# A quarter of W_out between W_in's chunks, v ahead of q for batch 1, and a new order of steps, in a packed attention and MLP kernel

## The chip, the cores and the metric

The kernel runs on one core of a Trainium2 chip. The metric is the device time of one execution in microseconds (us). The core has a matrix engine (TensorE, "PE" in the profile; its weight loads are "PEld"), a vector engine (VectorE, "DVE"), an activation engine (ScalarE, "ACT"), GpSimd ("POOL") and a queue engine (SyncE, "SP"). Each takes its instructions in the order of the program and waits by semaphores for the others. Loads from device memory go through 16 DMA engines, which all queues share.

## The reference

Two attentions stand one after the other, then an MLP. In the first attention 32 packed queries per head read 576 keys and values; in the second the 576 queries read the 32 results, as keys and as values. The heads are put side by side and go through the MLP with a squared Relu.

```python
def sm_attn(qq, kk, vv):
    s = scale * np.matmul(qq, kk.transpose(0, 1, 3, 2))
    ...
    return np.matmul(a, vv)
p_packed = sm_attn(p, k, v)
out = sm_attn(q, p_packed, p_packed)
...
h = x @ w_in
r = np.maximum(h, 0.0)
g = s * (r * r) + b
return (g @ w_out).astype(np.float32)
```

Batch 8, heads 8, sequence 576, head size 64; x has 4608 rows of 512; W_in is 512 x 2048 and W_out 2048 x 512. Inputs and output are float32.

## The kernel before

Matmuls run in bf16; the loads on GpSimd's queue convert from float32 as they go. The eight batches are worked off one after another, but their steps are mixed: while the attention of batch b + 1 runs, the last product of batch b fills the gaps of TensorE. The mixing is written out by hand, as a list of words (lines 663 to 690) that `run` (line 569) turns into calls. All instructions are pinned: the order of the words is the order on every engine. What the words mean, with their functions:

- `Lk`, `Lq`, `Lv`, `Lp`, `Lwi`, `Lwo`: issue a load on GpSimd's queue (lines 115 to 143). `Lwi0` to `Lwi3` are the four chunks of W_in, of 512 columns each; `Lwo0` to `Lwo3` the four quarters of W_out, each four of its 16 blocks of rows. One is 512 KB in bf16, a batch's k, q or v 576 KB. k, q and v have one raw buffer each, so batch 1's may come only when batch 0's has been read.
- `Tk b.h`, `Tq b.h` (`on_pe`, line 189): transpose half of the heads of k or q on TensorE, then copy to SBUF. For batches 2 to 7 `Dk` and `Dq` do it by a DMA of SyncE's queue.
- `V` (`order_v`, line 220): DVE reorders v. `F b.a` (`first_scores`): first scores of half of the heads, and Exp on ACT. `P` (`packed`): their product with v, then a reciprocal and two scalings on DVE. `X` (`turned`): transposes the result, `ppd`.
- `S` (`second_scores`), `A b.x` (`weights`, and `weights_half` for batch 0): second scores, Exp, sums by a matmul with ones, Ln, Exp of minus that, and the product on DVE that gives aT. For batch 0 this last product is the word `G` (line 340), by halves of the rows.
- `W b.c` (`packed_w`, line 356): ppd times chunk c of W_in (for later batches two chunks), which is the MLP's first weight with the second attention's values folded in. It is copied from PSUM to `pw` by ACT (first part) and DVE (second part). For batch 0's chunk 0 DVE copies it in two halves, the second at the word `E`.
- `M b.m` (`mlp_in`, line 430): 4 matmuls aT times block m of pw, a Relu to `rlu` (on ACT; on DVE for batch 0 where m % 4 == 2), and the square to gT on DVE. `h 0.m.f` (`mlp_in_half`) is the same for two blocks and half of the rows; h0.0.0 has its Relu on DVE.
- `O b.t x n` (`Out.step`, line 498): n of the 16 matmuls of an output tile of 128 rows, gT times a block of W_out. Step m needs gT's block m and W_out's quarter m // 4. After the sixteenth DVE scales it and adds the bias, and SyncE stores it.
- `BT`, `BC` (lines 462 and 477): column sums of W_out for the bias; BT reads all four quarters. `PA`, `PPA`: the same preparation of p for batches 2 to 7 at once; `PD`, `PP` for one batch.
- `Z n` and `Y n`: fillers, n matmuls of 512 columns on a tile of zeros. `Z` (line 551) writes to a PSUM tile of its own, `Y` (line 558) to the buffer that the next step will use.

PSUM: the steps T, PP, F, S, A, M, h, BT, BC and W of later batches share two buffers of two banks (`psh`, tag h, shown as `hps`); a step may start only when the copy or Relu of the step two before has read its buffer. O, P, Z and W of batch 0 share four buffers of one bank.

The order of the opening's loads on GpSimd's queue before the change, behind batch 0's k, p, v and q: `Lwi0 Lwi1 Lwi2 Lwi3 Lwo0 Lwo1 Lp1 Lk1 Lq1 Lv1 Lwo2 Lwo3 Lpall Lk2`.

Of the kernel before, what the change touches and what calls it, by code (L numbers as in the profile page):

```python
# [14 lines left out]
def kernel(  # L15
# [45 lines left out]
    def mm(*a, **kw):  # L61
        return tc.keep_in_program_order(nc.tensor.matmul(*a, **kw))  # L62
# [367 lines left out]
    def mlp_in(b, m):  # L430
        hps = big()
        for a in range(2):
            for hf in range(2):
# [7 lines left out]
        rlu = ysp.tile([P, 2, HS], BF16, tag="rlu", name="rlu")
        if b == 0 and m % 4 == 2:
            vec.tensor_scalar_max(out=rlu[:], in0=hps[:, :, 0:HS], scalar1=0.0)
        else:
            act.activation(out=rlu[:], in_=hps[:, :, 0:HS], func=AF.Relu)
# [1 line left out]
        vec.tensor_tensor(
            out=gT[:, m, g0:g0 + S].rearrange("p (a s) -> p a s", a=2),
            in0=rlu[:], in1=rlu[:], op=ALU.mult,
        )  # L450
# [212 lines left out]
    for word in """
        Lwi0 Lwi1 Lwi2 Lwi3 Lwo0 Lwo1 Lp1 Tk0.0 Z10 PD Tk0.1 Lk1 PP0 Z3 F0.0 V0.0 F0.1 Z5 P0.0 V0.1 P0.1
        Z2 Tq0.0 Z1 X0 Z1 Tq0.1 Lq1 Lv1 Lwo2 Lwo3 Lpall Z4 S0 Z3 A0.0 W0.0 Z1 A0.1 G0.0 E Z1 h0.0.0 W0.1
        G0.1 h0.2.0 Y2 h0.0.1 h0.2.1 W0.2 M0.4 W0.3 M0.5 M0.6 O0.0x1 M0.7 O0.0x3 M0.8 M0.9 O0.1x1 PD1
        O0.0x1 M0.10 M0.11 O0.0x3 O0.1x1 PP1 M0.12 O0.1x2 Tk1.0 Tk1.1 Lk2 O0.1x2 M0.13 O0.1x1 F1.0
        O0.1x1 Tq1.0 O0.2x1 Tq1.1 O0.2x1 F1.1 O0.2x2 V1 Lv2 Lq2 M0.14 P1.1 M0.15 O0.2x3 O0.0x2 X1 O0.0x2
        O0.1x1 S1 O0.1x3 O0.2x1 BT PA A1.0 O0.0x3 BC A1.1 O0.1x3 O0.2x3 W1.0 O0.0x1 O0.1x1 O0.2x5 W1.2
        V2 O0.3x6 M1.0 PPA M1.1 M1.2 Dq2 Dk2 Lk3 Lv3 Lq3 O0.3x9 M1.3 M1.4 O0.3x1 O1.0x1 M1.5 M1.6 O1.0x2  # L670
        M1.7 M1.8 O1.0x2 M1.9 M1.10 O1.0x2 M1.11 M1.12 O1.0x2 M1.13 M1.14 O1.0x2 M1.15 O1.0x2 F2.0 F2.1
        O1.0x3 O1.1x3 P2.1 O1.1x5 X2 O1.1x3 S2 O1.1x4 A2.0 O1.1x1 O1.2x1 A2.1 O1.2x7 W2.0 O1.2x8 O1.3x1
        V3 O1.3x1 W2.2 O1.3x6 M2.0 O1.3x1 M2.1 O1.3x1 M2.2 O1.3x1 M2.3 Dq3 Dk3 Lk4 Lv4 Lq4 O1.3x1 M2.4
        O1.3x1 M2.5 O1.3x1 M2.6 O1.3x1 M2.7 O1.3x1 M2.8 O1.4x1 M2.9 O1.4x1 M2.10 O1.4x1 M2.11 O1.4x1
        M2.12 O1.4x1 M2.13 O1.4x1 M2.14 O1.4x1 M2.15 O1.4x9 O2.0x6 F3.0 F3.1 O2.0x6 P3.1 O2.0x4 O2.1x1
        X3 O2.1x5 W3.0 O2.1x6 W3.2 O2.1x4 O2.2x2 S3 O2.2x4 A3.0 O2.2x2 V4 A3.1 O2.2x8 O2.3x8 M3.0 M3.1
        Dq4 Dk4 Lk5 Lv5 Lq5 O2.3x2 M3.2 M3.3 O2.3x2 M3.4 M3.5 O2.3x2 M3.6 M3.7 O2.3x2 M3.8 M3.9 O3.0x2
        M3.10 M3.11 O3.0x2 M3.12 M3.13 O3.0x2 M3.14 M3.15 O3.0x8 F4.0 F4.1 O3.0x2 O3.1x4 P4.1 O3.1x5 X4
        O3.1x3 S4 O3.1x4 A4.0 O3.2x2 A4.1 O3.2x7 W4.0 O3.2x7 O3.3x2 V5 W4.2 O3.3x6 M4.0 O3.3x2 M4.1 M4.2
        O3.3x2 M4.3 Dq5 Dk5 Lk6 Lv6 Lq6 O3.3x4 M4.4 M4.5 O3.4x2 M4.6 M4.7 O3.4x2 M4.8 M4.9 O3.4x2 M4.10  # L680
        M4.11 O3.4x2 M4.12 M4.13 O3.4x2 M4.14 M4.15 O3.4x6 O4.0x6 F5.0 F5.1 O4.0x6 P5.1 O4.0x4 O4.1x1 X5
        O4.1x5 S5 O4.1x4 A5.0 O4.1x2 A5.1 O4.1x4 O4.2x3 W5.0 O4.2x7 V6 O4.2x5 W5.2 O4.2x1 O4.3x5 M5.0
        M5.1 O4.3x2 M5.2 Dq6 Dk6 Lk7 Lv7 Lq7 M5.3 O4.3x2 M5.4 M5.5 O4.3x2 M5.6 M5.7 O4.3x2 M5.8 M5.9
        O4.3x2 M5.10 M5.11 O4.3x1 O5.0x1 M5.12 M5.13 O5.0x2 M5.14 M5.15 O5.0x12 F6.0 F6.1 O5.0x1 O5.1x5
        P6.1 O5.1x5 X6 O5.1x3 S6 O5.1x3 O5.2x1 A6.0 O5.2x2 A6.1 O5.2x7 W6.0 O5.2x6 O5.3x3 V7 W6.2 O5.3x6
        M6.0 O5.3x2 M6.1 M6.2 O5.3x2 M6.3 Dq7 Dk7 M6.4 O5.3x2 M6.5 M6.6 O5.3x1 O5.4x1 M6.7 M6.8 O5.4x2
        M6.9 M6.10 O5.4x2 M6.11 M6.12 O5.4x11 M6.13 M6.14 O6.0x2 M6.15 O6.0x5 F7.0 F7.1 O6.0x6 P7.1
        O6.0x3 O6.1x2 X7 O6.1x4 S7 O6.1x4 A7.0 O6.1x2 A7.1 O6.1x4 O6.2x3 W7.0 O6.2x12 W7.2 O6.2x1 O6.3x5
        M7.0 M7.1 O6.3x2 M7.2 M7.3 O6.3x2 M7.4 M7.5 O6.3x2 M7.6 M7.7 O6.3x2 M7.8 M7.9 O6.3x2 M7.10 M7.11
        O6.3x1 O7.0x1 M7.12 M7.13 O7.0x2 M7.14 M7.15 O7.0x13 O7.1x16 O7.2x16 O7.3x16 O7.4x16  # L690
    """.split():
# [31 lines left out]
```

## Time and profile before

| what | value |
|---|---|
| time, median of 5 runs (lowest to highest) | 250.99 us (250.51 to 251.53) |
| the profiled execution | 250.56 us |
| its span from first to last instruction | 248.8 us |
| TensorE busy | 239.1 us (96%) |
| DVE busy | 144.3 us (58%) |
| ACT busy | 138.9 us (56%) |
| fillers to their own tile (zps), in the mean 435 ns as shown | 43, 13.0 us |
| granted TensorE clock, mean | 0.998 |

Busy time is what the records cover. A matmul's end is modelled and the next one starts before it: 512 columns are shown as some 380 ns, while six of them in a row start 0.216 us apart. So a step is best priced by the starts of what comes before and after it. The idle time before an instruction stands in brackets in the timeline, with what ended it. The chain that ended last lies on TensorE for 86% of the span, on DMAs for 10%.

### The profile page before, as it was taken

To read this page: it belongs to the slowest core of one execution; us is meant where nothing else is said; L and a number is where in the kernel's file an instruction comes from. 1 tells how busy PE (TensorE), PEld (TensorE's weight loads), DVE (VectorE), ACT (ScalarE), POOL (GpSimd) and SP (SyncE) were. 2 spreads that over 40 slices of the span, in tenths; PEclk is the share of its full clock that TensorE was granted. 3 is DMA by queue.
4 is the path that set the end of the run, shared out by engine and by line. 5 is a ranking of instruction groups with operands and counts; after the bars stand their busy time and mean duration, and the time that the engine had idled before them with its cause. 6 is when DMAs were issued, how large, how long until landed. Compare 5 with 4: busy or idle time off the path is not lost.

```text
span 248.8 us, 5498 instructions
## 1 busy us (share of the span) xinstructions
PE 239.1 (96%) x2291; PEld 132.3 (53%) x2291; DVE 144.3 (58%) x278; ACT 138.9 (56%) x218; POOL 29.1 (12%) x43
## 2 busy tenths in 40 slices
PE   7796999999999999999999999999999999999994
PEld 2452566356643665356544655466545654366453
DVE  4438768498629573567548662677347642767221
ACT  2156743558846882568655763678375844577000
POOL 8633212000300030000300030001200000000000
PEclk9999999999999999999999999999999999999999
DMA  3999999999498869429898969368995911121133
GB/s 32 198 206 206 203 204 206 195 218 209 83 205 188 196 109 220 105 56 140 152 220 177 206 80 222 89 127 134 171 232 144 145 42 45 42 46 42 42 87 86
DMA packets 59450, 35.50 MB, mean 143 GB/s; under 512 B 32160, under 2 KB 54944, under 8 KB 59424
## 3 DMA queue, kind: packets, MB, share of 16 engines
q0 software_dynamic: 25184, 18.61, 50.1%
q1 hardware_dynamic: 34192, 16.49, 29.3%
q8 instruction: 18, 0.29, 0.5%
q14 instruction: 8, 0.07, 0.1%
q10 hardware_dynamic: 48, 0.03, 0.0%
HBM read 37.23 MB, written 9.44 MB: 188 GB/s over the span
## 4 chain that ended last, share of the span: by engine, by line
PE 86%; DMA 10%; ACT 1%; DVE 1%; issue 0%; POOLq 0%
PE yps L62 49%; PE hps L62 31%; DMA vn<-in_v_dram 8%; DMA kn<-in_k_dram 2%; PE zps L62 2%; PE pps L62 2%; PE hps L65 1%; PE pps L65 1%; ACT e L73 1%; DVE vr L73 0%; DVE aT L73 0%; ACT pbd L73 0%; ACT rcd L73 0%; ACT ld L73 0%; PE tps L65 0%
## 5 line engine op out<-in xcount | busy, mean ns | idle before, releaser
L62 PE MATMUL yps<-w_out_sb,gT 128*128 128x512 bf16 (+1 forms) x592 | 146.1, 374 | 0.3 <-DMA w_out_sb<-in_moe_w_out_dram 0.3
L73 ACT ACTIVATE rlu<-hps 128x576 bf16<-128x576 f32 x124 | 75.6, 649 | 28.7 <-PE hps L62 25.9
L62 PEld LDWEIGHTS <-gT 128*128 128x128 bf16 x592 | 54.8, 98 | 49.5 <-issue 7.4
L62 PE MATMUL hps<-aT,pw 128*128 128x288 bf16 x512 | 76.4, 286 | 2.4 <-DVE aT L73 2.3
L73 DVE TENSOR_TENSOR gT<-rlu 128x576 bf16<-128x576 bf16 x128 | 58.0, 458 | 31.1 <-ACT rlu L73 27.5
L62 PEld LDWEIGHTS <-pw 128*128 128x128 bf16 x512 | 49.4, 97 | 29.6 <-issue 4.5
L73 DVE SCALAR_TENSOR_TENSOR ysb<-yps,svec,biasrep 128x512 f32<-128x512 f32 (+1 forms) x37 | 26.9, 732 | 22.4 <-PE yps L62 19.3
L73 ACT ACTIVATE e<-hps 96x768 bf16<-96x768 f32 (+2 forms) x34 | 21.8, 693 | 29.9 <-PE hps L62 29.7
L73 ACT CAST pw<-hps 128x1024 bf16<-128x1024 f32 x14 | 14.2, 1012 | 16.5 <-PE hps L62 16.0
L73 DVE TENSOR_TENSOR aT<-e,rcd 128x576 bf16<-128x576 bf16 x16 | 12.1, 757 | 18.0 <-ACT rcd L73 18.0
L73 POOL DMA_DIRECT2D kn<-in_k_dram x9 | 6.9, 767 | 129.5 <-DMA kT<-kn 100.5
L73 DVE CAST pw<-hps 128x1024 bf16<-128x1024 f32 x14 | 17.0, 1217 | 2.7 <-PE hps L62 2.7
L62 PE MATMUL zps<-zb 128*128 128x512 bf16 x43 | 13.0, 435 | 1.2 <-DVE zb L73 1.2
L73 ACT ACTIVATE ld<-hps 128x576 f32<-128x576 f32 x16 | 10.3, 643 | 2.3 <-PE hps L62 1.6
L73 ACT ACTIVATE rcd<-ld 128x576 f32<-128x576 f32 x16 | 10.9, 683 | 0.5
L62 PEld LDWEIGHTS <-ppd 64*32 64x32 bf16 x384 | 3.6, 89 | 10.3 <-issue 6.9
L62 PE MATMUL hps<-w_in_sb,ppd 64*32 64x512 bf16 x224 | 8.8, 381 | 0.0
L73 DVE RECIPROCAL rd<-pps 128x2 f32<-128x2 f32 x8 | 1.4, 170 | 12.6 <-PE pps L62 12.6
L62 PEld LDWEIGHTS <-kT 128*128 128x128 bf16 x192 | 6.9, 98 | 2.4 <-issue 0.6
L73 DVE COPY vr<-vn 96x3072 bf16<-96x3072 bf16 (+1 forms) x9 | 7.7, 859 | 0.3 <-DMA vn<-in_v_dram 0.3
L62 PEld LDWEIGHTS <-zb 128*128 128x128 bf16 x45 | 4.4, 109 | 6.3 <-issue 3.1
L73 POOL DMA_DIRECT2D vn<-in_v_dram x9 | 6.8, 753 | 6.1 <-DVE vr L73 4.6
(58 smaller groups left out, 100.7 us busy)
## 6 DMA issues: line engine op xcount, KB each, us to landing
out_dram<-ysb SPq DMA_DIRECT2D x23, 192.0 KB, 2.6
kn<-in_k_dram POOLq DMA_DIRECT2D x7, 576.0 KB, 6.2
qn<-in_q_dram POOLq DMA_DIRECT2D x7, 576.0 KB, 12.5
vn<-in_v_dram POOLq DMA_DIRECT2D x7, 576.0 KB, 10.0
out_dram<-ysb SPq DMA_DIRECT2D x24, 128.0 KB, 2.5
w_in_sb<-in_moe_w_in_dram POOLq DMA_DIRECT2D x4, 512.0 KB, 13.6
w_out_sb<-in_moe_w_out_dram POOLq DMA_DIRECT2D x4, 512.0 KB, 18.9
out_dram<-ysb SPq DMA_DIRECT2D x23, 64.0 KB, 2.0
```

Of the source, the lines that this page charges most:

```text
L62: return tc.keep_in_program_order(nc.tensor.matmul(*a, **kw))
L65: return tc.keep_in_program_order(nc.tensor.transpose(*a, **kw))
L73: return lambda *a, **kw: tc.keep_in_program_order(f(*a, **kw))
```

## The change

Three things change. First, the loads: `Lwo0` goes ahead of `Lwi2`, and `Lv1` ahead of `Lq1` (and to an earlier place in the list, behind `V0.1`). Second, the list of words has a new order; in the opening there is one filler Z less, and there are 14 fillers Y in place of 2. Of batch 0's steps the h come as h0.0.0, h0.2.0, h0.2.1, h0.0.1; W0.1 stands behind G0.1 and h0.2.0; W0.2 and W0.3 stand two M each later; the first O stands behind M0.11; M0.14 and M0.15 ahead of V1. In batches 2, 5 and 6 W b.0 stands ahead of S, and the M and O of batches 1 to 7 are mixed a little differently. All words of the computation are there as often as before. Third, the Relu and the square of `mlp_in` and `mlp_in_half` become one function, `squared`; and the branch in `packed_w` for chunk 0 asks for batch 0 too.

```diff
-            if ch == 0:
+            if b == 0 and ch == 0:
...
+    def squared(out, hps, on_vec):
+
+        h = hps[:, :, 0:HS]
         rlu = ysp.tile([P, 2, HS], BF16, tag="rlu", name="rlu")
-        if hf == 0 and m == 0:
-            vec.tensor_scalar_max(out=rlu[:], in0=hps[:, :, 0:HS], scalar1=0.0)
+        if on_vec:
+            vec.tensor_scalar_max(out=rlu[:], in0=h, scalar1=0.0)
         else:
-            act.activation(out=rlu[:], in_=hps[:, :, 0:HS], func=AF.Relu)
-        g0 = slot(b) * S + hf * HS
-        vec.tensor_tensor(out=gT[:, m:m + 2, g0:g0 + HS], in0=rlu[:], in1=rlu[:], op=ALU.mult)
+            act.activation(out=rlu[:], in_=h, func=AF.Relu)
+        vec.tensor_tensor(out=out, in0=rlu[:], in1=rlu[:], op=ALU.mult)
...
-        Lwi0 Lwi1 Lwi2 Lwi3 Lwo0 Lwo1 Lp1 Tk0.0 Z10 PD Tk0.1 Lk1 PP0 Z3 F0.0 V0.0 F0.1 Z5 P0.0 V0.1 P0.1
-        Z2 Tq0.0 Z1 X0 Z1 Tq0.1 Lq1 Lv1 Lwo2 Lwo3 Lpall Z4 S0 Z3 A0.0 W0.0 Z1 A0.1 G0.0 E Z1 h0.0.0 W0.1
-        G0.1 h0.2.0 Y2 h0.0.1 h0.2.1 W0.2 M0.4 W0.3 M0.5 M0.6 O0.0x1 M0.7 O0.0x3 M0.8 M0.9 O0.1x1 PD1
-        O0.0x1 M0.10 M0.11 O0.0x3 O0.1x1 PP1 M0.12 O0.1x2 Tk1.0 Tk1.1 Lk2 O0.1x2 M0.13 O0.1x1 F1.0
-        O0.1x1 Tq1.0 O0.2x1 Tq1.1 O0.2x1 F1.1 O0.2x2 V1 Lv2 Lq2 M0.14 P1.1 M0.15 O0.2x3 O0.0x2 X1 O0.0x2
-        O0.1x1 S1 O0.1x3 O0.2x1 BT PA A1.0 O0.0x3 BC A1.1 O0.1x3 O0.2x3 W1.0 O0.0x1 O0.1x1 O0.2x5 W1.2
-        V2 O0.3x6 M1.0 PPA M1.1 M1.2 Dq2 Dk2 Lk3 Lv3 Lq3 O0.3x9 M1.3 M1.4 O0.3x1 O1.0x1 M1.5 M1.6 O1.0x2
+        Lwi0 Lwi1 Lwo0 Lwi2 Lwi3 Lwo1 Lp1 Tk0.0 Z10 PD Tk0.1 Lk1 PP0 Z3 F0.0 V0.0 F0.1 Z5 P0.0 V0.1 Lv1
+        P0.1 Z1 Tq0.0 Z1 X0 Z1 Tq0.1 Lq1 Lwo2 Lwo3 Lpall Z3 S0 Z3 A0.0 Z1 W0.0 A0.1 G0.0 E Y8 h0.0.0
+        G0.1 Z1 h0.2.0 Z1 W0.1 Y4 h0.2.1 Y1 h0.0.1 Y1 M0.4 M0.5 W0.2 M0.6 M0.7 W0.3 M0.8 M0.9 M0.10
+        M0.11 PD1 O0.0x4 M0.12 M0.13 O0.0x2 PP1 O0.0x2 Tk1.1 Tk1.0 Lk2 O0.1x2 M0.14 O0.1x1 M0.15 V1 Lv2
+        O0.1x2 F1.0 F1.1 O0.1x3 O0.2x3 P1.1 Tq1.0 Tq1.1 Lq2 X1 O0.2x5 O0.0x2 S1 O0.0x2 O0.1x2 A1.0
+        O0.1x2 BT PA A1.1 O0.0x3 O0.1x2 BC O0.1x1 O0.2x3 W1.0 O0.0x1 O0.1x1 O0.2x4 W1.2 V2 O0.2x1 O0.3x5
+        M1.0 M1.1 O0.3x2 M1.2 M1.3 Dq2 Dk2 Lk3 Lv3 Lq3 PPA M1.4 M1.5 O0.3x9 M1.6 O1.0x1 M1.7 O1.0x1 M1.8
...
```

More of the change, by code (lines that the diff above doesn't have):

```diff
@@ L421, in mlp_in_half @@
                 )
+        g0 = slot(b) * S + hf * HS
+        squared(gT[:, m:m + 2, g0:g0 + HS], hps, hf == 0 and m == 0)
+    def squared(out, hps, on_vec):
+        h = hps[:, :, 0:HS]
         rlu = ysp.tile([P, 2, HS], BF16, tag="rlu", name="rlu")
-        if hf == 0 and m == 0:
-            vec.tensor_scalar_max(out=rlu[:], in0=hps[:, :, 0:HS], scalar1=0.0)
-        else:
-            act.activation(out=rlu[:], in_=hps[:, :, 0:HS], func=AF.Relu)
-        g0 = slot(b) * S + hf * HS
-        vec.tensor_tensor(out=gT[:, m:m + 2, g0:g0 + HS], in0=rlu[:], in1=rlu[:], op=ALU.mult)
+        if on_vec:
+            vec.tensor_scalar_max(out=rlu[:], in0=h, scalar1=0.0)
+        else:
+            act.activation(out=rlu[:], in_=h, func=AF.Relu)
+        vec.tensor_tensor(out=out, in0=rlu[:], in1=rlu[:], op=ALU.mult)
     def mlp_in(b, m):
@@ L440, in mlp_in @@
                 )
[L441 to L445, printed above, removed]
         g0 = slot(b) * S
[L447 to L450, printed above, removed]
+        squared(gT[:, m, g0:g0 + S].rearrange("p (a s) -> p a s", a=2), hps, b == 0 and m % 4 == 2)
     bias = {}
@@ L669 @@
-        O0.1x1 S1 O0.1x3 O0.2x1 BT PA A1.0 O0.0x3 BC A1.1 O0.1x3 O0.2x3 W1.0 O0.0x1 O0.1x1 O0.2x5 W1.2
-        V2 O0.3x6 M1.0 PPA M1.1 M1.2 Dq2 Dk2 Lk3 Lv3 Lq3 O0.3x9 M1.3 M1.4 O0.3x1 O1.0x1 M1.5 M1.6 O1.0x2
-        M1.7 M1.8 O1.0x2 M1.9 M1.10 O1.0x2 M1.11 M1.12 O1.0x2 M1.13 M1.14 O1.0x2 M1.15 O1.0x2 F2.0 F2.1
-        O1.0x3 O1.1x3 P2.1 O1.1x5 X2 O1.1x3 S2 O1.1x4 A2.0 O1.1x1 O1.2x1 A2.1 O1.2x7 W2.0 O1.2x8 O1.3x1
-        V3 O1.3x1 W2.2 O1.3x6 M2.0 O1.3x1 M2.1 O1.3x1 M2.2 O1.3x1 M2.3 Dq3 Dk3 Lk4 Lv4 Lq4 O1.3x1 M2.4
@@ L674 @@
[L674 to L688, printed above, removed]
@@ L689 @@
-        M7.0 M7.1 O6.3x2 M7.2 M7.3 O6.3x2 M7.4 M7.5 O6.3x2 M7.6 M7.7 O6.3x2 M7.8 M7.9 O6.3x2 M7.10 M7.11
-        O6.3x1 O7.0x1 M7.12 M7.13 O7.0x2 M7.14 M7.15 O7.0x13 O7.1x16 O7.2x16 O7.3x16 O7.4x16
+        Lwi0 Lwi1 Lwo0 Lwi2 Lwi3 Lwo1 Lp1 Tk0.0 Z10 PD Tk0.1 Lk1 PP0 Z3 F0.0 V0.0 F0.1 Z5 P0.0 V0.1 Lv1
+        P0.1 Z1 Tq0.0 Z1 X0 Z1 Tq0.1 Lq1 Lwo2 Lwo3 Lpall Z3 S0 Z3 A0.0 Z1 W0.0 A0.1 G0.0 E Y8 h0.0.0
+        G0.1 Z1 h0.2.0 Z1 W0.1 Y4 h0.2.1 Y1 h0.0.1 Y1 M0.4 M0.5 W0.2 M0.6 M0.7 W0.3 M0.8 M0.9 M0.10
@@ new lines @@
+        M0.11 PD1 O0.0x4 M0.12 M0.13 O0.0x2 PP1 O0.0x2 Tk1.1 Tk1.0 Lk2 O0.1x2 M0.14 O0.1x1 M0.15 V1 Lv2
+        O0.1x2 F1.0 F1.1 O0.1x3 O0.2x3 P1.1 Tq1.0 Tq1.1 Lq2 X1 O0.2x5 O0.0x2 S1 O0.0x2 O0.1x2 A1.0
+        O0.1x2 BT PA A1.1 O0.0x3 O0.1x2 BC O0.1x1 O0.2x3 W1.0 O0.0x1 O0.1x1 O0.2x4 W1.2 V2 O0.2x1 O0.3x5
+        M1.0 M1.1 O0.3x2 M1.2 M1.3 Dq2 Dk2 Lk3 Lv3 Lq3 PPA M1.4 M1.5 O0.3x9 M1.6 O1.0x1 M1.7 O1.0x1 M1.8
+        O1.0x1 M1.9 O1.0x1 M1.10 O1.0x1 M1.11 O1.0x1 M1.12 O1.0x1 M1.13 O1.0x1 M1.14 O1.0x1 M1.15 O1.0x4
@@ new lines @@
+        F2.0 F2.1 O1.0x3 O1.1x3 P2.1 O1.1x5 X2 O1.1x3 W2.0 O1.1x5 O1.2x1 W2.2 O1.2x6 S2 O1.2x4 A2.0
+        O1.2x2 A2.1 O1.2x1 V3 O1.2x2 O1.3x11 M2.0 M2.1 O1.3x2 M2.2 Dq3 Dk3 Lk4 Lv4 Lq4 M2.3 O1.3x2 M2.4
+        M2.5 O1.3x1 O1.4x1 M2.6 M2.7 O1.4x2 M2.8 M2.9 O1.4x2 M2.10 M2.11 O1.4x2 M2.12 M2.13 O1.4x2 M2.14
+        M2.15 O1.4x7 O2.0x6 F3.0 F3.1 O2.0x5 P3.1 O2.0x5 X3 O2.1x6 S3 O2.1x4 A3.0 O2.1x2 A3.1 O2.1x4
+        O2.2x3 W3.0 O2.2x6 V4 O2.2x6 W3.2 O2.2x1 O2.3x5 M3.0 M3.1 O2.3x1 Dq4 Dk4 Lk5 Lv5 Lq5 O2.3x1 M3.2
@@ new lines @@
+        M3.3 O2.3x2 M3.4 M3.5 O2.3x2 M3.6 M3.7 O2.3x2 M3.8 M3.9 O2.3x2 M3.10 M3.11 O2.3x1 O3.0x1 M3.12
+        M3.13 O3.0x2 M3.14 M3.15 O3.0x10 F4.0 F4.1 O3.0x3 O3.1x3 P4.1 O3.1x5 X4 O3.1x3 S4 O3.1x4 A4.0
+        O3.1x1 O3.2x1 A4.1 O3.2x7 W4.0 O3.2x8 O3.3x1 V5 O3.3x1 W4.2 O3.3x6 M4.0 O3.3x1 M4.1 O3.3x1 M4.2
+        O3.3x1 M4.3 Dq5 Dk5 Lk6 Lv6 Lq6 O3.3x1 M4.4 O3.3x1 M4.5 O3.3x1 M4.6 O3.3x1 M4.7 O3.3x1 M4.8
+        O3.4x1 M4.9 O3.4x1 M4.10 O3.4x1 M4.11 O3.4x1 M4.12 O3.4x1 M4.13 O3.4x1 M4.14 O3.4x1 M4.15 O3.4x9
@@ new lines @@
+        O4.0x5 F5.0 F5.1 O4.0x6 P5.1 O4.0x5 X5 O4.1x6 W5.0 O4.1x6 S5 O4.1x4 A5.0 O4.2x2 A5.1 O4.2x7 W5.2
+        V6 O4.2x6 M5.0 O4.2x1 M5.1 O4.3x1 M5.2 O4.3x1 M5.3 O4.3x1 Dq6 Dk6 Lk7 Lv7 Lq7 M5.4 O4.3x1 M5.5
+        O4.3x1 M5.6 O4.3x1 M5.7 O4.3x1 M5.8 O4.3x1 M5.9 O4.3x1 M5.10 O4.3x1 M5.11 O4.3x1 M5.12 O4.3x1
+        M5.13 O4.3x1 M5.14 O4.3x1 M5.15 O4.3x2 O5.0x14 F6.0 O5.0x2 F6.1 O5.1x5 P6.1 O5.1x5 X6 O5.1x3
+        W6.0 O5.1x3 O5.2x3 S6 O5.2x4 A6.0 O5.2x2 A6.1 O5.2x7 W6.2 V7 O5.3x6 M6.0 O5.3x4 M6.1 M6.2 O5.3x2
@@ L691 @@
+        M6.3 Dq7 Dk7 M6.4 O5.3x2 M6.5 M6.6 O5.3x2 M6.7 M6.8 O5.4x2 M6.9 M6.10 O5.4x2 M6.11 M6.12 O5.4x2
+        M6.13 M6.14 O5.4x2 M6.15 O5.4x8 O6.0x6 F7.0 F7.1 O6.0x6 P7.1 O6.0x4 O6.1x1 X7 O6.1x5 S7 O6.1x4
+        A7.0 O6.1x2 A7.1 O6.1x4 O6.2x3 W7.0 O6.2x12 W7.2 O6.2x1 O6.3x5 M7.0 M7.1 O6.3x2 M7.2 M7.3 O6.3x2
+        M7.4 M7.5 O6.3x2 M7.6 M7.7 O6.3x2 M7.8 M7.9 O6.3x2 M7.10 O6.3x1 M7.11 O7.0x1 M7.12 O7.0x1 M7.13
+        O7.0x1 M7.14 O7.0x1 M7.15 O7.0x12 O7.1x16 O7.2x16 O7.3x16 O7.4x16
     """.split():
```

## The prediction

> **What bounds the kernel now.** I read first the windows view (busy time by stretch), then who TensorE waited for, then the timelines of the opening. The columns of the windows are the stretch in us, the busy time of each engine with its instructions, the granted clock, the DMA share and GB/s.
>
> ```profile
> 17.42:28.51 11.09, 8.43 (x88) 4.06 (x88) 7.49 (x15) 8.21 (x16) 3.06 (x4) 1.00 1.24 207
> 28.51:41.16 12.65, 11.99 (x126) 7.95 (x126) 9.28 (x19) 6.09 (x11) 1.76 (x2) 1.00 1.31 203
> 49.86:244.60 194.74, 194.74 (x1799) 108.29 (x1799) 114.41 (x209) 115.47 (x179) 11.47 (x15) 1.00 0.71 134
> ```
>
> From 49.86 to 244.60 TensorE (first column) is busy for 194.74 of 194.74 us, at full clock, and from 50 on no wait of TensorE is listed at all. So nothing after the opening can be shortened by order. What the opening loses reaches the end one to one. In it the DMA engines move 203 to 207 GB/s without a pause: the landings are a fixed timetable of bytes.
>
> TensorE's waits in the first 70 us (total us, times, longest), and its timeline where it matters:
>
> ```profile
> PE hps L62 <- DVE aT L73: 2.3, 2, 1.2
> PE pps L62 <- DVE vr L73: 0.6, 1, 0.6
> PE yps L62 <- DMA w_out_sb<-in_moe_w_out_dram: 0.3, 1, 0.3
> ```
>
> ```profile
> 21.34 0.65 PE L62 MATMUL hps<-aT,pw 128*128 128x288 bf16 x4 [1.13 <-DVE aT L73]
> ...
> 24.60 1.14 PE L62 MATMUL hps<-aT,pw 128*128 128x288 bf16 x8 [1.17 <-DVE aT L73]
> ...
> 28.51 0.38 PE L62 MATMUL yps<-w_out_sb,gT 128*128 128x512 bf16 x1 [0.29 <-DMA w_out_sb<-in_moe_w_out_dram]
> ...
> 41.16 0.55 PE L62 MATMUL pps<-vr,e 96*32 96x65 bf16 x48 [0.58 <-DVE vr L73]
> ```
>
> The bracket is idle time, and what ended it. By starts of the matmuls the four gaps are 1.29, 1.33, 0.46 and 0.75 us (a matmul's shown end is later than the next one's start). The last is batch 1's v: GpSimd's timeline issues it at 21.40, it lands 18.7 us later (40.13), then DVE reorders it, and the Relu of M0.14 stood behind it:
>
> ```profile
> 40.15 0.96 DVE L73 COPY vr<-vn 96x3072 bf16<-96x3072 bf16 x1 [0.33 <-DMA vn<-in_v_dram]
> 41.03 0.75 DVE L73 TENSOR_SCALAR rlu<-hps 128x576 bf16<-128x576 f32 x1
> ```
>
> Landings are read from GpSimd's queue, where an issue waits for the load eight before it:
>
> ```profile
> 23.71 0.77 POOL L73 DMA_DIRECT2D w_out_sb<-in_moe_w_out_dram  x1 [1.54 <-DMA w_in_sb<-in_moe_w_in_dram]
> 26.21 0.75 POOL L73 DMA_DIRECT2D w_out_sb<-in_moe_w_out_dram  x1 [1.74 <-DMA w_in_sb<-in_moe_w_in_dram]
> 28.75 0.99 POOL L73 DMA_DIRECT2D pall<-in_p_dram  x1 [1.79 <-DMA w_out_sb<-in_moe_w_out_dram]
> ```
>
> Less the 0.28 us that an issue takes to start after its release, W_in's third chunk landed at 23.43, the fourth at 25.93, W_out's first quarter at 28.47: 2.5 us each. With the issue-to-landing times, W_out's second quarter is in at 31.20, batch 1's k at 34.27, q at 37.17, v at 40.13 (2.9 us each), W_out's third quarter at 42.63, its fourth at 45.14.
>
> **The loads.** No byte is added, so the timetable only swaps places: W_out's first quarter lands at 23.43, W_in's third chunk at 25.93, its fourth at 28.47; v at 37.17, q at 40.13; the rest stays. All issue waits of the new order end by 28.5 (v waits for W_in's first chunk, 18.70, which is earlier than its 21.40 now), and the queue is some ten us deep, so GpSimd hides them. The Trainium skill (DMA: Bandwidth & Descriptors, "Anatomy of one DMA — SWDGE (gpsimd) path") prices one such load at about 2.0 us plus its bytes at 436 GB/s, 3.2 us for 0.52 MB; by that the fourth chunk lands at 29.1, and the step W0.3 that needs it, and all behind it, comes some 0.6 later. The rows show 2.5 us apart in a full queue: the fixed part overlaps. I take 2.5.
>
> **Prices.** From the timelines: a 512-column matmul 0.216 (an O step, or a filler), a step M or h 0.49, a half transpose Tk or Tq 0.51, F 0.35, S 0.37, a single W 0.34, each change to or from a packed shape 0.09. M's start to its Relu's start 0.69 (24.60 to 25.29), Relu 0.65 on ACT, 0.75 on DVE, and 0.05 to the matmul that takes the buffer: with two hps buffers a pair of M costs 1.39, not 0.98, if nothing stands between. On DVE, queued back to back, a gT product takes 0.38, a cast 0.60, a Relu 0.67.
>
> **To W_in's fourth chunk (gain, then given back).** Two fillers fewer ahead of S0: it starts when qT is ready, 17.01 for 17.42. The chain of Exp, sums, Ln, Exp, aT then gives aT at 20.88 for 21.29. But the eight new fillers (Y8, 1.72) can only start when Ln has freed their buffer, 19.43, and end at 21.16: h0.0.0 starts there, 0.19 earlier than 21.34. W0.1's cast no longer stands ahead of aT's second half on DVE, so h0.2.1 starts at 23.87 for 24.60 (Y4 ends then). h0.0.1 follows at 24.57, M0.4 at 25.47, M0.5 at 25.96, W0.2 at 26.54, M0.6 at 26.89, M0.7 at 27.41. TensorE is done at 27.90 and waits for the fourth chunk: W0.3 from 28.51 to 28.85. At 28.51 the kernel before has done W0.3 (0.43) but not M0.7 (0.49), this one M0.7 but not W0.3. So the lead is gone, and W_out's early quarter is not used: its first step, O0.0x4, stands behind M0.11.
>
> **From there to P1.1 (a loss, then the v wait gone).** M0.6's Relu is on DVE and queues behind M0.5's product and W0.2's cast (28.37 to 29.12), so M0.8 starts at 29.17, not 28.85. M0.8 to M0.11 have no O between them now and run at the buffers' pace: M0.10 at 30.56, M0.11 at 31.11, end 31.60. O0.0x4 ends at 32.46; before, TensorE stood at 32.43 with two O more done: 0.43 lost. M0.12, M0.13, O, PP1, O to 34.41; Tk1.1 (k is in), then 0.23 of wait for the buffer that PP1's copies hold, Tk1.0 to 35.66. M0.14 and M0.15 end at 37.29; v is reordered behind their products at 39.5, hidden by O and F. P1.1 starts at 39.93 instead of 41.16. Tq1.0 then finds q (40.17) landed: the 0.75 of v's wait has no successor here.
>
> **From P1.1 to the dense part.** Tq1 to 41.44, X1 0.06 late behind pk, five O to 42.69 (third quarter in at 42.67), two O, S1, four O, A1.0, two O: BT at 45.39 against 45.42, fourth quarter in at 45.18. The same O counts are done on both sides (12, 12 and 8), and A1.0 (0.24) is done already; the change of shape behind BT that it paid falls to A1.1. Then the cost of A1.0's place: its aT product comes ahead of BT's copy on DVE, so BC waits until 47.87 for 47.69, and W1.0 starts at 49.79, for 49.86 before with the same work done. M1.1 follows M1.0 directly, and W1.2's cast on DVE holds its buffer some 0.1 longer. Net 0.07 less 0.12 plus 0.1 (F2.1 no longer meets M1.15's Relu, as four O steps stand between, not two): about **-0.1 us**.
>
> **Later batches.** Orders differ (W2 ahead of S2, one M per O in batches 1 and 5), but each pattern stands in the trace already without a stall: W ahead of S in batch 3, one M per O at 0.705 us in batch 2. Cost nothing, bounds -0.1 to +0.3. `squared` gives the same instructions.
>
> **Sum.** 250.56 (span 248.8 and 1.8 around it) less 0.1 is 250.5 for an execution like the profiled one. That one lies 0.4 under the median shown, 250.99, and as much under the mean of the five, 250.93. I forecast for a typical execution: 250.93 less 0.1, 250.8.
>
> **Rivals.** *Only the landings bind* (chance 0.22): DVE and buffers cost nothing behind W0.3, TensorE meets each landing, BT starts at 45.27 and BC doesn't wait: 0.15 + 0.24 + 0.1, some 0.5, hence 250.4. For: M0.8 waits only because of one queued cast. Against: four M in a row pay 1.39 a pair in the rows. *DVE's queue decides, slower* (0.23): from W0.2's cast to Tk1.0's copy DVE has 5.6 us of work in a row by the spacings above. If M0.6's Relu ends 0.7 later than 29.12, buffers pass it on to M0.8, M0.10, M0.12 and the k transposes, and no landing absorbs it, as P1.1 is already behind q and BT 0.2 behind W_out. It decides from the point where that Relu ends after 29.1, one to one; at 0.7, 251.5. For: the Relu behind `vr` at 41.03. Against: DVE had 1.05 idle at 25.97. *It does not do what it says* (0.10): the wait that counts is not v's but W_out's last quarter at 45.14, which no swap here moves; what is won at P1.1 is spent in front of BT, and BC, W1.0 and M1.1 wait as above: no change, 250.9. The forecast keeps 0.45.
>
> **Range and chances.** Something under 0.3% (0.75 us) can't be told from no change here; the five runs spread 1.0. The likeliest case alone spans 250.3 to 251.3; taking in the two outer cases, 250.0 to 251.6. Faster by over 0.3% needs the first rival and scatter: 0.12. Slower: most of the second, a little of the forecast: 0.20. Between: 0.68.
>
> **What would show it.** W0.3 at about 28.5 behind W_in's landing; M0.8 at 29.2 and M0.10 at 30.6 behind Relus; P1.1 near 39.9 with no wait for v; BT near 45.4; BC behind `biasrep`; W1.0 at 49.8; and no wait after 55. I am wrong if O0.0 starts before 31, if TensorE waits for q by more than 0.2, or if a wait appears in batches 2 to 7.

## The result, and the profile after

| | kernel before | changed kernel |
|---|---|---|
| median of the compared runs (lowest to highest) | 251.03 us (250.43 to 251.62), 80 runs | 250.54 us (250.34 to 251.34), 43 runs |
| the profiled execution | 250.56 us, span 248.8 | 250.60 us, span 248.8 |
| TensorE busy | 239.1 us | 241.5 us |

The ratio is 0.9984, 95% interval 0.9979 to 0.9990: some 0.4 us by the ratio and 0.5 between the medians, below the 0.75 us that the prediction held to be too small to tell from no change. So the answer is "the same", as forecast, within the range, with a gain larger than the forecast's 0.1.

Two things must be known to read so small a number. The two profiled executions differ by 0.04 us, not by 0.4: the gain lies between the medians and not between the profiles. The profile of the kernel before is of an execution 0.4 us faster than its usual one, that of the changed kernel of one 0.2 slower. (Of the changed kernel's 31 executions at full clock, 16 took 250.34 to 250.41 us and 15 took 250.50 to 250.60; all three of its profiles are of the second group.) And in about three of ten executions of either kernel the granted TensorE clock was 0.993 instead of 0.997 to 1.0, which costs 0.5 to 0.9 us, so that "at full clock" below means a median of executions at 0.997 or more: 250.95 to 250.99 before, 250.41 after.

The windows view of the changed kernel, on the stretches shown of before (stretch, us, busy time of TensorE, weight load, DVE, ACT, POOL, clock, DMA share, GB/s):

```profile
17.42:28.51 11.09, 10.56 (x80) 5.53 (x81) 7.50 (x16) 8.29 (x16) 3.06 (x4) 1.00 1.24 206
28.51:41.16 12.65, 12.21 (x179) 8.20 (x179) 10.12 (x22) 6.64 (x12) 2.53 (x3) 1.00 1.31 204
41.16:49.86 8.70, 8.08 (x69) 3.27 (x65) 4.48 (x9) 3.86 (x6) 0.77 (x1) 1.00 1.45 197
49.86:244.60 194.74, 194.74 (x1800) 108.33 (x1799) 113.92 (x209) 116.92 (x178) 11.47 (x15) 1.00 0.74 134
```

TensorE is "busier" ahead of 28.51, by 2.1 us, with fewer matmuls (80 for 88): those are the fillers Y, and busy time says nothing of progress here. From 49.86 to 244.60 it is full as before, with one matmul more in the same stretch. That it is full does not say that nothing changed in it, as the part on the later batches shows. The waits of TensorE from 5 to 70 us (what it wrote and its line, what it waited for, total us, times, longest), without two that both kernels have, for batch 0's k and for `pbd`:

```profile
PE wps L62 <- DMA w_in_sb<-in_moe_w_in_dram: 0.6, 1, 0.6
PE yps L62 <- DMA w_out_sb<-in_moe_w_out_dram: 0.5, 1, 0.5
PE hps L62 <- ACT rlu L73: 0.2, 1, 0.2
```

The waits for aT and for `vr` are gone from the list. Two are new (W_in's chunk and a Relu), one has moved from W_out's first quarter to its third. TensorE's timeline shows where (start, length, operation, and in brackets the idle time and what ended it):

```profile
28.71 0.41 PE L62 MATMUL wps<-w_in_sb,ppd 64*32 64x512 bf16 x8 [0.62 <-DMA w_in_sb<-in_moe_w_in_dram]
29.05 1.15 PE L62 MATMUL hps<-aT,pw 128*128 128x288 bf16 x8
30.45 1.19 PE L62 MATMUL hps<-aT,pw 128*128 128x288 bf16 x8 [0.25 <-ACT rlu L73]
...
39.74 0.56 PE L62 MATMUL pps<-vr,e 96*32 96x65 bf16 x48
40.24 1.19 PE L65 MATMUL hps<-identb,qn 96*128 96x96 bf16 x24
...
41.38 1.24 PE L62 MATMUL yps<-w_out_sb,gT 128*128 128x512 bf16 x5
43.14 0.59 PE L62 MATMUL yps<-w_out_sb,gT 128*128 128x512 bf16 x2 [0.51 <-DMA w_out_sb<-in_moe_w_out_dram]
...
45.67 1.05 PE L62 MATMUL hps<-w_out_sb,onesb 128*32 128x512 bf16 x16
...
48.25 1.09 PE L62 MATMUL hps<-biasrep,rowsf 128*128 128x512 f32 x2
```

P1.1 is at 39.74 without a wait: 1.42 us earlier than before. But five O behind 41.38 end, at 0.216 us each, at 42.46; the next starts at 43.14. That is a gap of 0.68 us by starts, for W_out's third quarter. BT is then at 45.67, where before it was at 45.42. The chain of waits names the same transfer (start, us, what):

```profile
23.75 19.35 DMA w_out_sb<-in_moe_w_out_dram
43.09 0.04 issue
43.14 0.59 PE yps L62 x2
```

W_out's third quarter landed at 43.09. The kernel before had it at 42.63, and the change moves no load behind v and q in the queue.

### The profile page after: what moved, and what is told of

Read it like the earlier page. It is cut to its first block, busy times and chain, and to the rows that moved or that the text cites. A ratio compares the mean times of both kernels' runs of the same rounds, so it can differ in the third digit from the quotient of the medians.

```text
span 248.8 us, 5518 instructions
## 1 busy us (share of the span) xinstructions
PE 241.5 (97%) x2302; PEld 133.5 (54%) x2302; DVE 144.1 (58%) x278; ACT 140.5 (56%) x218; POOL 29.1 (12%) x43
## 4 chain that ended last, share of the span: by engine, by line
PE 81%; DMA 16%; issue 1%; POOL 0%; DVE 0%; POOLq 0%
PE yps L62 49%; PE hps L62 30%; DMA w_out_sb<-in_moe_w_out_dram 14%; DMA kn<-in_k_dram 3%; PE pps L62 1%; PE pps L65 1%; POOL kn L73 0%; DVE ysb L73 0%; POOL identb L73 0%; POOLq L73 0%; POOLq L705 0%
## 5 line engine op out<-in xcount | busy, mean ns | idle before, releaser
L62 PE MATMUL yps<-w_out_sb,gT 128*128 128x512 bf16 (+1 forms) x592 | 147.8, 374 | 0.5 <-DMA w_out_sb<-in_moe_w_out_dram 0.5
L73 ACT ACTIVATE rlu<-hps 128x576 bf16<-128x576 f32 x124 | 77.0, 649 | 23.2 <-PE hps L62 20.0
L62 PE MATMUL hps<-aT,pw 128*128 128x288 bf16 x512 | 78.3, 286 | 0.2 <-ACT rlu L73 0.2
L62 PE MATMUL zps<-zb 128*128 128x512 bf16 x42 | 13.6, 452 | 1.2 <-DVE zb L73 1.2
L62 PEld LDWEIGHTS <-zb 128*128 128x128 bf16 x56 | 5.5, 107 | 7.2 <-issue 3.2
```

The lines of the kernel that those rows point to most:

```text
L73: return lambda *a, **kw: tc.keep_in_program_order(f(*a, **kw))
```

## The experiments

All runs are timed against the kernel before on the same chip. Fillers multiply zeros and give nothing to the output, so no variant leaves out a part of the computation.

### The changed kernel again

No edit.

> The changed kernel itself, on another chip or at another time, to see how far its executions differ. Both theories expect 0.998 to 0.999 of the kernel before. The theory of order (v's wait removed, then W_in's, q's and W_out's landings bind) expects the same stations as in the changed kernel's profile: W0.3 at 28.7, Tq1.0 at 40.2, BT at 45.3 to 45.7. The theory of the clock expects that executions of over 251 us go with a mean granted clock of about 0.993 and those under 250.7 with 0.998 or more, in both kernels, and that the share of low clocks is lower in the changed one.

Median 250.59 us (14 runs), ratio 0.9988 [0.9977, 1.0000]; at full clock 250.50. Its profile, at 250.58 us, has W_out's third quarter late in the same way. The sizes repeat to 0.1 us, and that is what can be told apart below. All its executions over 251 us had the clock 0.993, as expected; but they are not rarer than in the kernel before (6 of 14 here, 14 of 48 there).

### W_out's first quarter back behind W_in

```diff
-        Lwi0 Lwi1 Lwo0 Lwi2 Lwi3 Lwo1 Lp1
+        Lwi0 Lwi1 Lwi2 Lwi3 Lwo0 Lwo1 Lp1
```

> The changed kernel with W_out's first quarter behind W_in's fourth chunk again, v still ahead of q. If W0.3's wait of 0.78 us is on the path, the time falls by 0.6 to 0.8 us against the changed kernel (ratio to before 0.995 to 0.996). If the next landing, q's at 40.2, catches what is won (Tq1.0 already waits 0.12 for it), W0.3 starts at 27.9 without a wait, P1.1 earlier than 39.7, but Tq1.0 stays at 40.2 and the time stays within 0.1 us of the changed kernel (0.998). I expect the second.

Median 250.55 us (21 runs), ratio 0.9985 [0.9976, 0.9994]; at full clock 250.39 for 250.41. Nothing. Its TensorE timeline shows how the gain is lost:

```profile
27.97 0.41 PE L62 MATMUL wps<-w_in_sb,ppd 64*32 64x512 bf16 x8
28.78 1.14 PE L62 MATMUL hps<-aT,pw 128*128 128x288 bf16 x8 [0.40 <-ACT rlu L73]
...
34.33 1.19 PE L65 MATMUL hps<-identb,kn 96*128 96x96 bf16 x24
```

W0.3 (first line) starts 0.74 us earlier and waits for no landing. M0.8 (second) is only 0.27 earlier, since it now waits for a Relu. Tk1.1 (third) is 0.05 earlier, since batch 1's k lands at 34.29. P1.1 is at 39.70 for 39.74, and BT at 45.67 as in the changed kernel. The wait of 0.6 us that is new in TensorE's list was worth nothing. So the first of the two swaps of loads has no effect, of either sign, that could be told here.

### v behind q again

```diff
-        ... V0.1 Lv1 P0.1 ... Tq0.1 Lq1 Lwo2
+        ... V0.1 P0.1 ... Tq0.1 Lq1 Lv1 Lwo2
```

> The changed kernel with batch 1's q ahead of its v again, all else as changed. If v's landing is what the change moves, P1.1 waits until v is reordered, 41.2 instead of 39.7; of these 1.4 us some 0.5 go into the wait for W_out's third quarter, and the time rises by about 0.9 us against the changed kernel (ratio to before 1.002). If the swap doesn't matter, no change (0.998).

Median 251.25 us (13 runs), ratio 1.0008 [1.0000, 1.0016]; at full clock 251.25, that is 0.84 us slower than the changed kernel. The timeline:

```profile
38.34 1.46 PE L62 MATMUL yps<-w_out_sb,gT 128*128 128x512 bf16 x6
41.21 0.55 PE L62 MATMUL pps<-vr,e 96*32 96x65 bf16 x48 [1.41 <-DVE vr L73]
41.70 1.19 PE L65 MATMUL hps<-identb,qn 96*128 96x96 bf16 x24
```

Six O from 38.34 are done at 39.64, and P1.1 starts at 41.21, as it did in the kernel before (41.16). All of the new order's lead in the opening ends at this landing. In this order v ahead of q decides; the rest of the change without it is slower than the kernel before, by 0.3 us at full clock and at the edge of the interval.

### Without the fillers Y

```diff
-        ... G0.0 E Y8 h0.0.0 G0.1 Z1 h0.2.0 Z1 W0.1 Y4 h0.2.1 Y1 h0.0.1 Y1 M0.4
+        ... G0.0 E h0.0.0 G0.1 Z1 h0.2.0 Z1 W0.1 h0.2.1 h0.0.1 M0.4
```

> The changed kernel without its 14 fillers Y. By the theory of order h0.0.0 starts when aT is ready, 20.9 instead of 21.2, all that is won is spent in front of W_in's fourth chunk at 28.7, and the time stays (0.998). By the theory of the clock the fillers hold the granted clock in the thin stretch from 19.5 to 25.5; without them more executions have a mean clock near 0.993 and take 0.5 to 1 us longer (1.000 to 1.002).

Median 250.21 us (11 runs), ratio 0.9973 [0.9962, 0.9984]; at full clock 250.19. The clock was full as often as in the changed kernel (9 of 11 executions). The steps up to h0.2.1 came 0.2 to 0.3 us earlier, M0.4 0.5, and W0.3 waited for its chunk until 28.68 all the same: so far as the alternative had it. But the time fell by 0.2 at full clock, and by 0.4 between the medians of this run and of the unedited one above. The chain of waits of this profile shows the reason, in the row that stood at 19.35 us:

```profile
23.88 18.86 DMA w_out_sb<-in_moe_w_out_dram
42.74 0.04 issue
42.78 0.59 PE yps L62 x2
```

The third quarter landed at 42.74, 0.35 us earlier, and TensorE went on at 42.78 for 43.14. All that follows keeps those 0.36: BT 45.32, W1.0 49.79, last O step of the kernel 244.75 for 245.12. Both expectations missed: what the fillers cost in these two profiles was not time on TensorE but the landing of a load of the same size, at the same place in the same queue.

Why did it move? The instructions themselves come by DMA. The transfers of 40.9 to 41.2 us, first of the changed kernel, then of this one (queue, kind, packets, MB, share of 16 engines):

```profile
q0 software_dynamic: 67, 0.06, 123.8%
q8 instruction: 1, 0.02, 18.6%
```

```profile
q0 software_dynamic: 73, 0.06, 132.8%
```

One packet of 16 KB at 41.00, and 18.6% of 16 engines over 0.3 us is 0.89 us on one engine. In this kernel it comes at 41.50. A load is shared out to 16 engines, and its landing is that of the last share. In the trace's semaphore records of the third quarter the last three shares are in at 42.56, 42.71 and 43.09 in the changed kernel, here at 41.70, 42.70 and 42.74.

The fillers count as instructions, so their number sets when this packet comes. The theory from here on: it holds up one share of the third quarter. Behind 41.75 us three shares come in in the changed kernel and two without the Y, so one share more is late, and the landing moves by 0.35 us. The trace does not say on which engine a packet runs, so this much is a theory.

### Fewer fillers Z

`Z10` and `Z3` taken out ahead of the first scores, `Z5` made `Z4`, the Y kept.

```diff
-        Tk0.0 Z10 PD Tk0.1 Lk1 PP0 Z3 F0.0 V0.0 F0.1 Z5 P0.0
+        Tk0.0 PD Tk0.1 Lk1 PP0 F0.0 V0.0 F0.1 Z4 P0.0
```

> The changed kernel with 14 fillers Z fewer ahead of P0.0 (Z10 and Z3 out, Z5 cut to Z4), all Y kept: as many TensorE instructions as without the Y. If the fetch of TensorE's instructions by the DMA engines, which falls at 41.0 us in the changed kernel and at 41.5 without the Y, is what makes one sixteenth of W_out's third quarter late, the quarter lands at 42.7 and the time falls as without the Y, by 0.35 us against the changed kernel (ratio to before 0.9970 to 0.9975). If the Y themselves matter, by what they take in front of h0.0.0 and h0.2.1, the quarter stays at 43.1 and the time at 0.9985.

Median 250.54 us (9 runs), ratio 0.9975 [0.9963, 0.9987]. None of the nine executions had the full clock (0.984 to 0.986 in eight, 0.993 in one). The windows of its profile, in steps of 3.41 us:

```profile
4.80:8.21 3.41, 1.60 (x16) 0.73 (x14) 0.03 (x1) 0.00 (x0) 2.96 (x5) 1.00 1.15 165
8.21:11.62 3.41, 1.81 (x24) 1.64 (x24) 2.15 (x4) 0.73 (x2) 2.49 (x4) 0.50 1.37 199
11.62:15.03 3.41, 3.19 (x60) 2.02 (x60) 0.56 (x1) 1.50 (x2) 1.50 (x3) 0.50 1.30 203
```

TensorE was busy for only half of each of the first two stretches (second number, 1.60 and 1.81 of 3.41), and the clock was half in the stretch behind each. So the fillers Z do hold the clock. But the packet came at 41.99, the third quarter landed at 42.62, and with two stretches at half clock the time was still that of the changed kernel (250.54 for 250.54). What the clock cost was made up by something else, of which the earlier landing is one part.

### Two ways of using what was won

BC waits until 48.25 because A1.0's product stands ahead of BT's copy on DVE:

```profile
46.75 0.76 DVE L73 TENSOR_TENSOR aT<-e,rcd 128x576 bf16<-128x576 bf16 x1 [4.03 <-ACT rcd L73]
47.42 0.68 DVE L73 COPY biasrep<-hps 128x512 f32<-128x512 f32 x1
```

So the next kernel leaves the Y out and moves A1.0 behind BT and A1.1 behind BC; the one after that has W_out's first quarter behind W_in as well (the edit shown above).

```diff
-        ... O0.1x2 A1.0 O0.1x2 BT PA A1.1 O0.0x3 O0.1x2 BC O0.1x1 O0.2x3 W1.0
+        ... O0.1x2 O0.1x2 O0.2x1 BT PA A1.0 O0.0x3 BC A1.1 O0.1x3 O0.2x2 W1.0
```

> The changed kernel without the 14 Y and with A1.0 behind BT again (one O0.2 step in its place): BC then doesn't stand behind aT's product on DVE. If TensorE is bound behind BT by its own work and that wait, BT stays at 45.3 (W_out's fourth quarter), BC starts without its 0.27 us of wait, W1.0 starts at 49.55 instead of 49.79, and the time falls by 0.2 to 0.25 us against the kernel without the Y (ratio to before 0.9963 to 0.9968). If W1.0 waits for the buffer of BC, it stays at 0.9973.

> The one above with W_out's first quarter behind W_in's fourth chunk again. W0.3 then needs no landing, but k's at 34.3 and q's at 40.2 catch what is won: same time as the one above within 0.05 us. If the wait for W_in's fourth chunk (1.2 us without the Y) is on the path, 0.4 us or more faster.

Medians 250.22 (15 runs, ratio 0.9971 [0.9961, 0.9980]) and 250.20 us (11, 0.9969 [0.9957, 0.9981]); at full clock 250.18 both, for 250.19 without the Y alone. No gain. The timeline of the second:

```profile
46.99 1.09 PE L62 MATMUL hps<-biasrep,rowsf 128*128 128x512 f32 x2
...
49.33 0.70 PE L62 MATMUL hps<-w_in_sb,ppd 64*32 64x512 bf16 x16
49.97 1.47 PE L62 MATMUL yps<-w_out_sb,gT 128*128 128x512 bf16 x6
51.36 0.96 PE L62 MATMUL hps<-w_in_sb,ppd 64*32 64x512 bf16 x16
52.26 1.47 PE L62 MATMUL yps<-w_out_sb,gT 128*128 128x512 bf16 x5
53.57 0.65 PE L62 MATMUL hps<-aT,pw 128*128 128x288 bf16 x4
```

BC's wait is gone, and W1.0 (second line) starts at 49.33, 0.46 earlier than without the Y alone. But W1.2 to the next O step takes 0.90 us by starts (51.36 to 52.26) where it took 0.59 there, and M1.0 is at 53.57 for 53.68: of 0.46 some 0.1 is left. DVE's timeline has the reason:

```profile
49.76 0.76 DVE L73 TENSOR_TENSOR aT<-e,rcd 128x576 bf16<-128x576 bf16 x1 [0.40 <-ACT rcd L73]
50.44 1.22 DVE L73 CAST pw<-hps 128x1024 bf16<-128x1024 f32 x1
```

The second part of W1.2 needs the buffer that this cast of W1.0 reads until 51.66, and the cast stands behind A1.1's product. In the trace W1.2's first matmul starts at 51.36 and its second, which waits for DVE, at 51.71. Without the Y alone the same cast starts at 50.55, 0.11 later, and that is all that is left of the 0.46.

### Single executions of both kernels

Kernel before three times and changed kernel once, no edit, to catch the execution of each that the medians stand for.

> The kernel before, for another profile of it: most of its executions at full clock take 250.9 to 251.0 us, and the profile shown of it was one of the few at 250.4 to 250.6. If the usual execution differs by a late landing, it shows TensorE waiting for W_out's third quarter (43.0 instead of 42.6) or for v (40.5 instead of 40.1), and 0.4 us more span at the same clock. If it differs by the clock, the granted clock differs and the landings stay. If the profile falls at 250.5 again, nothing is told.

> The kernel before once more, for a profile of its usual execution at full clock (250.9 to 251.0 us; 27 of 34 at full clock lay there, 5 near 250.43). The profile of 251.53 us showed half the clock from 8.06 to 11.47 us. If the usual execution loses its 0.5 us to a landing, v or a quarter of W_out lands some 0.4 later than in the first profile (40.13, 42.63, 45.14) and the stations behind it are later; if to the clock at the start, the stations before 20 us are later already.

> As the one before it: a second chance to see the usual execution; same expectations.

> The changed kernel once more, for a profile of its fastest group (250.34 to 250.41 us; the two profiles so far lay at 250.6). If W_out's third quarter is what parts the groups, it lands near 42.9 instead of 43.1 and the stations from there on are 0.2 us earlier; otherwise the difference lies ahead of it.

They took 251.53, 250.45, 250.50 and 250.57 us. The first is one with clock 0.993, and shows what that is:

```profile
4.64:8.06 3.42, 1.61 (x18) 0.88 (x17) 0.00 (x0) 0.00 (x0) 2.96 (x5) 1.00 1.13 159
8.06:11.47 3.41, 3.41 (x11) 1.19 (x9) 0.95 (x2) 0.00 (x0) 2.50 (x4) 0.50 1.37 199
11.47:49.86 38.39, 34.81 (x445) 20.30 (x451) 24.46 (x51) 21.22 (x38) 8.69 (x12) 1.00 1.32 204
```

One stretch of 3.41 us at half clock, behind one in which TensorE was busy for 1.61 us: it waits there for batch 0's k. The other two of before agree with its first profile to 0.1 us at BT and at the landings (v 40.03 and 40.08, third quarter 42.55 and 42.59). But the usual full-clock execution of before takes 250.95, and no profile of it was caught: all three with full clock lie in its fast tail. The changed kernel's profile was to be one of its faster group; at 250.57 us it is of the slower one, like the two before it, and has the third quarter late again, at 43.07. Whether the quarter is as late in the faster group is not known.

### Six fillers Y fewer

If the packet of instructions is what delays the third quarter, it is enough to move it: `Y8` becomes `Y2`, nothing else.

```diff
-        G0.0 E Y8 h0.0.0
+        G0.0 E Y2 h0.0.0
```

> The changed kernel with Y8 cut to Y2, the other six Y kept: 12 TensorE instructions fewer ahead of 21 us. Five profiles of kernels with the changed kernel's number of TensorE instructions have the fetch at 40.98 to 41.01 us and W_out's third quarter at 43.07 to 43.10; eight others, with 22 to 28 instructions fewer or more of them later, have it at 41.09 or later and the quarter at 42.53 to 42.74. If the place of the fetch decides, this one has it near 41.2, the quarter at or under 42.75, O0.0 behind it 0.35 earlier than in the changed kernel, and the time 0.35 us lower (ratio to before 0.9970 to 0.9975). If it is not the fetch but how W0.1, h0.2.1 and h0.0.1 stand with Y4, Y1 and Y1 between them, which are kept, the quarter stays at 43.1 and the time at 0.9985.

Median 250.08 us (18 runs), ratio 0.9968 [0.9958, 0.9979]; at full clock 250.05, 0.36 less than the changed kernel and 0.9 less than the kernel before. Its median is the lowest of all that ran, though the intervals of the three kernels without any Y overlap with its own. Its own profile fell into an execution with the stretch at half clock, so the early steps lie later there, and the packet came at 42.76, behind the landing; where it comes at full clock is not on record. The profile shows the third quarter in at 42.54 and TensorE passing that point without a wait:

```profile
42.41 0.28 PE L65 MATMUL pps<-identb,pk 128*128 128x128 bf16 x2
42.53 1.67 PE L62 MATMUL yps<-w_out_sb,gT 128*128 128x512 bf16 x7
44.13 0.44 PE L62 MATMUL hps<-qT,ppd 64*32 64x288 bf16 x16
```

All fourteen profiles in one table:

| kernels | packet starts, us | third quarter lands, us |
|---|---|---|
| changed kernel (3 profiles), W_out's quarter back, v behind q | 40.98 to 41.01 | 43.07 to 43.10 |
| kernel before (4 profiles) | 41.09 to 42.47 | 42.53 to 42.63 |
| without Y, without Y and A1.0 moved, with W_out's quarter back too, fewer Z, six Y fewer | 41.44 to 42.76 | 42.54 to 42.74 |

The split has no exception, and the one forecast made from it (the fall by 0.35 with six Y fewer) held. By this table alone the packet could still stand for something else: the kernel before, with its packet at 41.09, is only 0.08 away from the late group.

The landing records of all the loads say more. In the fourteen profiles 316 loads of this queue land between 7 and 55 us with all 16 shares on record. In 307 of them the number of shares that come over 0.7 us behind the middle one equals the number of 16 KB packets that have started by then: none ahead of the first packet (16.6 to 18.6 us), then one, two, three and four. The other nine are loads whose middle share came within 0.4 us behind a packet's start. So each packet leaves one more share late in the loads that follow, by some 1.0 to 1.25 us. The load that is in flight when the packet comes can land later still: the third quarter's last share lies 1.57 us behind its middle one in the changed kernel. With six Y fewer, where the packet came at 42.76, it is the fourth quarter that is late, at 45.53, the latest of all fourteen. That the packets make these shares late is thus shown by count and by time. Why a packet at 41.01 still catches the third quarter and one at 41.09 does not stays open.

## Why the prediction was right, and where not

**The whole.** "Same" held, and the landings swapped as on record. W_in's chunks came at 25.96 and 28.66 (25.93 and 28.47 predicted), v at 37.24 (37.17), q at 40.19 (40.13). The 2.5 us for each chunk or quarter, taken in place of the estimate of 3.2 from the Trainium skill (DMA: Bandwidth & Descriptors, "Anatomy of one DMA — SWDGE (gpsimd) path"), was right to 0.2 us there; W_out's third quarter, 2.9 behind q, is the exception. None of the three signs of being wrong came: O0.0 started at 31.48, Tq1.0 did not wait for q, and no wait is listed in batches 2 to 7.

**To W0.3.** S0 16.98 (17.01), h0.0.0 21.18 (21.16), h0.2.1 23.90 (23.87), W0.2 26.58 (26.54), then the wait for W_in's fourth chunk, W0.3 at 28.71 (28.51). Right, and so was "the lead is gone". That it does not matter, because k of batch 1 stands behind it as the next gate, was not said; the run with W_out's quarter moved back showed it.

**To P1.1.** The wait of M0.8 behind M0.6's Relu on DVE, predicted at 29.17, did not come: M0.8 started at 29.05, right behind W0.3. By the semaphores of the trace it waits for ACT alone, so it has the buffer that M0.7's Relu freed; it is M0.9 that waits for DVE and has M0.6's, and it starts only at 29.55. The two buffers are not taken strictly in turn, as the step assumed. M0.10 waited behind a Relu as predicted (30.45 for 30.56). The wait of 0.23 between the two transposes of k did not come (the O behind them starts at 35.44 for 35.66), and that is the lead with which P1.1 came, at 39.74 (39.93), without a wait for v. Tq1.0 followed 0.50 later, at 40.24 (40.42), with q in at 40.19; with q long landed, in the run with v behind q, the same step takes 0.49. "The 0.75 of v's wait has no successor here" held for this place.

**From P1.1 to the dense part: a step that failed.** "Five O to 42.69 (third quarter in at 42.67)" rested on "the rest stays" for the landings. The third quarter came at 43.09, not 42.63, and O went on at 43.14. Part of it was made up by a shorter way to BT (2.53 us from there for 2.70), the rest was carried on: BT 45.67 for 45.39, BC 48.25 for 47.87, W1.0 50.14 for 49.79. The wait of BC behind A1.0's product was where predicted. In the run without Y, with the quarter in at 42.74, BT came at 45.32, BC at 47.90 and W1.0 at 49.79, as predicted. So the term that the prediction left out is the packet of instructions, which it put at nothing: some 0.35 us at W1.0.

**Later batches: the other step that failed.** No wait, as predicted. But "nothing after the opening can be shortened by order" and "cost nothing" did not hold. At W1.0 both kernels have the same steps behind them, and the changed one comes 0.28 later; its last O step comes 0.05 later (245.12 for 245.07). So 0.23 us were won behind W1.0, where a loss of 0.12 and a gain of 0.1 were put. The gain lies between F3.0 and S7, which also stand behind the same steps in both. TensorE's timeline, two lines of the kernel before, then two of the changed one:

```profile
94.92 0.86 PE L62 MATMUL hps<-pbd,kT 128*128 128x64 bf16 x24
208.66 0.44 PE L62 MATMUL hps<-qT,ppd 64*32 64x288 bf16 x16
```

```profile
95.28 0.86 PE L62 MATMUL hps<-pbd,kT 128*128 128x64 bf16 x24
208.77 0.44 PE L62 MATMUL hps<-qT,ppd 64*32 64x288 bf16 x16
```

That is 113.74 us before and 113.49 after, for the same matmuls, and TensorE is shown as busy throughout both. Two more profiles of the kernel before give 113.72 and 113.73, six more with the new order 113.48 or 113.49. Which of the changes of order wins it was not tested (among them, W3.0 now stands behind S3, which the description of the change leaves out).

**The sum.** The terms of the prediction's net, 0.07 less 0.12 plus 0.1, make a gain of 0.05, which was rounded to 0.1. For an execution like the profiled one +0.04 was measured: the two misses, 0.35 lost and some 0.25 won, nearly cancel, so that it came so close was in part luck. For the typical execution the forecast was 250.8, by taking the same -0.1 off 250.93. There -0.4 was measured (-0.5 at full clock), so the step "less 0.1 for a typical execution" failed too. The typical execution of before is 0.4 us longer than the profiled one, the changed kernel's is 0.2 shorter. Where those 0.4 us of the kernel before lie stays open, since three profiles at full clock did not catch them. A guess that fits: its packet, at 41.09 to 41.21 in these profiles, comes a little earlier in most executions and makes the third quarter late there as well; the O step that needs the quarter at 42.80 would then wait some 0.3 us. v's landing, for which only the kernel before waits, is another.

**The rivals.** *Only the landings bind* gave 250.4, the number nearest to the measured median, but not by its mechanism: M0.10 and BC did wait behind ACT and DVE. *DVE's queue decides* was to hold from a Relu of M0.6 that ends after 29.1; it ended at 29.14, and nothing was passed on, as the buffer was wanted only at 29.55. *It does not do what it says* fell with the run that puts v behind q: 0.84 us. Its remark that what is won at P1.1 is spent ahead of BT was true here (BT 45.67 for 45.42 before), but by the third quarter's landing and not by the last one's.

## What to carry to other kernels

In an opening that is bound by loads, time won ahead of a landing that comes later is worth nothing: two of the edits here removed a wait of 0.3 to 0.6 us, and the next gates (k's landing, a Relu, an O step) took all or most of it. So price a moved load at the step where the next landing stands, and look for the last landing that binds. The program's own instructions are part of that traffic, and their packets shift with every instruction added or taken out ahead of them. And an engine that is shown as busy all the time can still lose time; compare two kernels at steps that stand behind the same work. Where a gain of half a per cent is the matter, lay the profiled execution against the distribution of times first: the profile may be of an execution that the median does not stand for.

## What the runs showed of the hardware

- Loading instructions takes part in the traffic of loads: packets of 16 KB, 0.89 to 0.98 us each while loads run, 8 to 16 us apart in the changed kernel's opening (16.79, 25.21, 41.00 and 48.77 us). Up to 15 us all 16 shares of a load land within 0.4 us of the middle one; then each packet leaves one more share about 1 us behind (307 of 316 loads).
- With a packet at 40.98 to 41.01 us, the 512 KB load in flight landed at 43.07 to 43.10, in every other profile at 42.53 to 42.74. The number of fillers 20 us earlier moves the packet.
- A half clock comes in stretches of 3.41 us, one (251.53 us in the kernel before, about 0.5 more than usual) or two (fewer Z). The Trainium skill (TensorE: Matmul & The Clock Gate, "What's actually happening") tells of a free-running window of 3413 ns, which fits; it puts the half clock behind an idle window. Here a window in which TensorE was busy for 1.60 or 1.61 us of 3.41 was enough.
- Two orders of the same matmuls, both shown as busy throughout, took 113.49 and 113.74 us.
